# Linear attention and MLP: w_in loaded in even and odd partitions, its sums built in the first chunk on VectorE and GpSimd, late blocks of batch 1 in a tile of their own

## The chip, the cores and the metric

The kernel runs on one core of a Trainium2 chip. The core's engines work side by side, each with its own instruction stream: TensorE (PE, matmuls, with weight loads shown as PEld), VectorE (DVE), ScalarE (ACT), GpSimd (POOL) and SyncE (SP, which here issues DMA transfers). A tile on the core lies in SBUF, in 128 partitions; PE writes its results to PSUM, which has eight banks of 2 KB a partition. The metric is the device time of one execution in microseconds (us); the kernel before was run three times and its median counts.

## What is computed

Eight batches of eight heads with 576 positions of 64 elements go through a linear attention whose features are scaled with cosine and sine of the position. Its output, 4608 tokens of 512, goes through an MLP with 2048 hidden units.

```python
def _attn_ref(q, k, v):
    theta = np.pi / 2.0 * np.arange(S) / S
    def phi(x, c, s):
        r = np.maximum(x, 0.0)
        return np.concatenate([r * c, r * s], axis=-1)
    q_p, k_p = phi(q, cos_w, sin_w), phi(k, cos_w, sin_w)
    kv = np.einsum('bhsf,bhsd->bhfd', k_p, v)
    z = np.sum(k_p, axis=2)
    num = np.einsum('bhsf,bhfd->bhsd', q_p, kv)
    den = np.einsum('bhsf,bhf->bhs', q_p, z)[..., None] + 1e-06
    return num / den

def _moe_ref(x, w_in, w_out, beta):          # x: (4608, 512)
    h = x @ w_in                             # w_in: (512, 2048)
    g = h * (1.0 / (1.0 + np.exp(-beta * h)))
    return g @ w_out                         # w_out: (2048, 512)
```

## The kernel before

**Chunks and batches.** The MLP works on nine chunks of 512 tokens (c = 0 to 8), the attention on eight batches of 576 tokens, nine blocks of 64 each; chunk 0 is blocks 0 to 7 of batch 0, chunk 1 begins with block 8 of batch 0 and goes on with blocks 0 to 6 of batch 1, and so on. While PE does the MLP of one chunk, the other engines prepare the attention of the batch that the next chunk needs.

**A batch.** Raw q, k and v are loaded (`load_raw`, tiles `raw_q`, `raw_k`, `raw_v`, one of each, so that a load waits until the batch before has been read). `q_relu` and `k_relu` make bf16 tiles `qb` and `rk`, `v_scale` makes `vb` (v by cosine and by sine, with ones for the denominators). q is turned, either on PE (`q_turn_pe`, batches 0 and 1) or by a transposing DMA from SP (`q_turn_dma`), into `qt`; `tan_mul` multiplies it by the tangent into `qs`. `kv_mm` makes the 72 small matmuls of a batch's kv, `num_mm` multiplies q with it, `x_rden` and `x_mul` divide by the denominators into `xs`, and `x_turn_pe` or `x_turn_dma` turns that into `xt`, the left side of the MLP.

**The MLP.** h is made in 16 row tiles `jt` of 128 hidden units (`h_mm`, `h_group`), ACT computes silu(beta h) from it (`h_act`), and o is made from that with a w_out that is divided by beta. Weights come in fp32 pieces to four stage tiles (`load_w`), and are cast to bf16: `cast_win` into `win`, `cast_out` into `wout`, the latter with `rbeta`. From chunk 1 on o is made by a seven-product scheme (`o_fast`, later `o_pair`), which needs sums of w_out (`T1`, `T2`, `T3`, `T4`, made by `w_sums` in chunk 1) and sums of the activations (`S1` to `S4`); from chunk 3 on h is made the same way (`h_pair`), which needs four sums for each pair of row tiles of w_in (`wh_sum`, four of them in `wh_sums`, each a 128x256 subtraction or addition; eight pairs) and of x (`x_sum`).

**Order.** The schedule is by hand: instructions run on each engine in the order of the program, and wait for data by semaphores. Chunk 0 is a list of 32 slots: 4 to 15 are one row tile of h each, 16 to 23 are quarters of o, and 24 to 31 are one k step of o for all four token tiles. Work of batch 1 hangs on slots in the table `early`, work of batch 2 on slots of chunk 1. From chunk 2 on a string per chunk (`ORDERS`) gives the order, one word an operation: `W51` is sum 1 of pair 5 of `wh_sum`. SP issues loads in the order of the program too. Nearly all DMAs of the first 45 us go through it.

**In chunk 0**, DVE casts w_in's four quarters as they land (L115), does the last block of batch 0, casts eight row tiles of w_out (L123), scales v (L219), and takes k's and q's relu (L193); GpSimd and ACT take a share of the casts (L113). PE's h tiles wait for `win`, its o slots for `wout` (L544), and slot 22 ends with batch 1's `kv_mm` (L276). Between chunk 1's h and its o, ACT makes the two relus of batch 3's q (L192), in front of the copies of the first products out of PSUM (L602), which the products behind them wait for (L563).

The few lines that set this order:

```python
    22: lambda: (kv_mm(1, 0, 6), kv_mm(1, 1, 6), kv_take((0, 1), 6, "act"), q_relu(1, 1, "act", 5)),
    23: second,
    ...
    q_relu(3, 0, "act")
    q_relu(3, 1, "act")
    q_turn_dma(3)
    ...
    ops(x, "1 c1")
    one_sums(1)
    ops(y, "1 c1")
```

Of the kernel before, what the change touches and what calls it, by code (L numbers as in the profile page):

```python
# [16 lines left out]
P = 128  # L17
# [5 lines left out]
def kernel(  # L23
# [51 lines left out]

    def load_raw(b, name, j0=0, j1=4):
        js = slice(j0, j1)
        src = {"q": q, "k": k, "v": v}[name][b]
        nc.sync.dma_start(  # L79
            out=raw_tile(b, name)[:, js].rearrange("q j n d -> q j (n d)"),  # L80
            in_=src.rearrange("(j g) (p n) d -> (g p) j (n d)", g=2, n=NQ)[:, js, :])
# [8 lines left out]
    S1, S2, S3, S4 = (const.tile([P, JT // 2, TCH // 2], BF16, name=f"S{i}") for i in (1, 2, 3, 4))  # L90
    w_in_v = moe_w_in.rearrange("(j p) f -> p j f", p=P)
# [3 lines left out]
    def load_w(kind, i, step=4):  # L95
# [3 lines left out]
        for a in range(0, 4, step):  # L99
            if kind == "out":  # L100
                nc.sync.dma_start(out=st[:, a : a + step], in_=w_out_v[:, 4 * i + a : 4 * i + a + step, :])
                continue
            nc.sync.dma_start(out=st[:, a : a + step], in_=w_in_v[:, a : a + step, i * 512 : (i + 1) * 512])

    def cast_win(i, gj, eng="dve", f0=0, f1=512, jps=slice(0, 2)):

        g, jj = gj
        o = win[i].rearrange("q (jp g) f -> q jp g f", g=2)[jj * HP : (jj + 1) * HP, jps, g, f0:f1]
        a = stages["in", i].rearrange("q (jp jj) f -> q jp jj f", jj=2)[g * HP : (g + 1) * HP, jps, jj, f0:f1]
# [16 lines left out]
    GJ = [(0, 0), (0, 1), (1, 0), (1, 1)]  # L126

    load_raw(0, "q", 0, 2)
    load_raw(0, "q", 2, 4)
    beta16 = const.tile([JT, P], FP32, name="beta16")  # L130
    nc.scalar.dma_start(out=beta16, in_=moe_beta.rearrange("(j p) -> j p", p=P))
# [12 lines left out]
    zeros = S1.rearrange("q i t -> q (i t)")[:, 0:512]  # L144
# [50 lines left out]
    def q_relu(b, jp, eng="dve", n0=0, n1=NQ):  # L195
        return relu(qb[:, jp, n0:n1].rearrange("q n (j d) -> q j n d", j=2),
                    raw_tile(b, "q")[:, 2 * jp : 2 * jp + 2, n0:n1], eng)

    def k_relu(b, j0=0, j1=4, eng="dve", n0=0, n1=NQ):
        relu(rk.rearrange("q n j d -> q j n d")[:, j0:j1, n0:n1], raw_tile(b, "k")[:, j0:j1, n0:n1], eng)  # L200

    def v_scale(b, cs, jp=None, n0=0, n1=NQ, eng="dve"):
        t = (cos9, sin9)[cs]
        rv = raw_tile(b, "v")
        js = slice(0, 4) if jp is None else slice(2 * jp, 2 * jp + 2)
# [21 lines left out]
    def q_turn_pe(b, jp, bank, hold=False):  # L227

        parts = ((0, 0, 5), (1, 5, NQ))
# [40 lines left out]
    def kv_mm(b, jp, bank, jjs=(0, 1)):  # L270
        t = kv_out(jp, bank)
        for n in range(NQ):
            for jj in jjs:
                for g in range(2):
                    hs = slice(g * HP, (g + 1) * HP)
                    nc.tensor.matmul(  # L276
                        t[jj * HP : (jj + 1) * HP, g], lhsT=rk[hs, n, 2 * jp + jj, :],
                        rhs=vb[hs, n, 2 * jp + jj].rearrange("q s e -> q (s e)"),
# [10 lines left out]

    def num_mm(b, n, jp, bank, slot):  # L290

        for cs in range(2):
            for jj in range(2):
                rows = slice(jj * HP, (jj + 1) * HP)
                for g in range(2):
# [3 lines left out]
                        lhsT=(qts[b % 2], qs_of(b))[cs][rows, jp, n, cols],  # L299
# [15 lines left out]
    def x_mul(got, n0, n1):  # L315
        nv, rden, first, jps = got
        a, z, w = n0 - first, n1 - first, len(jps)
        o = xs[:, n0:n1, jps[0] : jps[-1] + 1].rearrange("q n s (j d) -> q j n s d", j=2)
# [6 lines left out]
    def x_mul_act(got, n):  # L325
        nv, rden, first, jps = got
        for s_, jp in enumerate(jps):
            for jj in range(2):
                nc.scalar.activation(xs[:, n, jp, jj * D : (jj + 1) * D], nv[:, jj, n - first, s_, 0:D],
# [67 lines left out]
    def g_sum(c, i0, i1, kind):  # L397

        k_ = i0 // 2
        g_e, g_o = (gs[c, k_][:, 2 * (i0 - 2 * k_) + r : 2 * (i1 - 2 * k_) : 2] for r in range(2))  # L400
        hf = TCH // 2
        A11, A12, A21, A22 = g_e[:, :, 0:hf], g_o[:, :, 0:hf], g_e[:, :, hf:TCH], g_o[:, :, hf:TCH]
        s1, s2, s3, s4 = (t[:, i0:i1] for t in (S1, S2, S3, S4))
# [18 lines left out]
    def wx_tiles():  # L422

        wx["w"] = stage.tile([P, 4, 512], FP32, name="w_stage", tag="w_stage").rearrange("q a f -> q (a f)").bitcast(
            BF16).rearrange("q (k s g f) -> q k s g f", k=4, s=4, g=2)
        wx["v"] = stage.tile([P, 4, 512], FP32, name="w_stage", tag="w_stage").rearrange("q a f -> q (a f)").bitcast(
            BF16).rearrange("q (k s g f) -> q k s g f", k=4, s=4, g=2)
# [5 lines left out]
    def w_sum(jt, i):  # L433
        return wx["w" if jt % 4 == 0 else "v"][:, jt // 4, i]

    def wh_sum(jt, kind):
# [6 lines left out]
        return nc.vector.tensor_tensor(o, l, r, op=op)  # L443

    def wh_sums(jt):
        for kind in (1, 3, 2, 4):
            got = wh_sum(jt, kind)
        return got
# [107 lines left out]
    def o_fast(c, pr, banks):  # L556
# [27 lines left out]
        def stored(key, op):  # L584
# [11 lines left out]
            "5": lambda: prod(e_ps, s_part(S1), T1, True, False),  # L596
            "6": lambda: prod(b_ps, s_part(S2), T2, False, False),
            "2": lambda: prod(a_ps, g_part(1, 0), B21, True, True),
            "7": lambda: prod(b_ps, s_part(S3), T3, False, False),
            "3": lambda: prod(e_ps, s_part(S4), B22, False, True),  # L600
# [11 lines left out]
    def o_pair(c, pr):  # L612
# [52 lines left out]
        lefts = (g_part(0, 0), s_part(S1), s_part(S2), g_part(1, 0), s_part(S3), s_part(S4), g_part(1, 1))  # L665
# [19 lines left out]
    warm_pe(58, 48)  # L685
# [7 lines left out]
    for bank, n0, n1 in ((6, 0, 5), (7, 5, NQ)):  # L693
        nc.vector.tensor_copy(tanr[:, n0:n1, :].rearrange("q n p -> q (n p)"), ps[:, bank, 0 : (n1 - n0) * HP])
# [47 lines left out]
    for gj, eng in zip(GJ, ("pool", "dve", "pool", "dve")):  # L742
        cast_win(0, gj, eng, jps=slice(0, 1))
    for gj, eng in zip(GJ, ("act", "pool", "pool", "pool")):
        cast_win(0, gj, eng, jps=slice(1, 2))
# [10 lines left out]
    def cast_halves(i, fs=(0, 256)):  # L756
        for f in fs:
            for gj in GJ:
                cast_win(i, gj, "pool" if i > 1 and gj == GJ[3] else "dve", f, f + 256)

    cast_halves(1)

    def rest():

        cast_halves(2)
        cast_halves(3)
        x_mul(x_rden(2, 0, 8, NQ, (0, 1)), 8, NQ)
# [3 lines left out]
        load_raw(1, "k")  # L771
# [320 lines left out]
```

## Time and profile before

| | us |
|---|---|
| median of three runs (273.26 to 273.82) | 273.54 |
| the profiled execution, its own time | 274.44 |
| its span, from the first to the last instruction | 272.7 |
| mean granted TensorE clock, share of full speed | 0.998 |

The page has a row for each engine's busy time as a share of the span, a chain of work that ended last, followed back from the last instruction, and groups of instructions by line. In a row, `L115 DVE CAST win<-w_stage 64x512 bf16<-64x512 f32 x20` is line 115 on VectorE, which makes `win` from `w_stage`, 64 partitions by 512 elements, twenty times. A timeline row begins with its start and its length in us and may end with idle time before it and what ended that; in a row of groups, busy time and the mean of one in ns follow the count; in a row of one line, shortest, median and longest in ns. Busy time by stretch of the span, with the share of DMA engines in use and what they moved:

```profile
20.00:30.00 10.00, 10.00 (x64) 4.53 (x62) 9.50 (x21) 8.43 (x13) 2.91 (x4) 1.00 1.05 388
30.00:38.00 8.00, 8.00 (x45) 3.53 (x47) 6.76 (x20) 6.48 (x13) 0.00 (x0) 1.00 1.05 391
50.50:70.20 19.70, 18.74 (x330) 10.32 (x328) 18.07 (x37) 16.57 (x28) 4.74 (x8) 1.00 1.06 304
```

The columns are the stretch, its length, busy us (and instructions) of PE, PEld, DVE, ACT and POOL, the granted clock, the DMA share and GB/s. The pieces of the loads landed one after the other: w_in's quarters at 16.39 (the first one's second half), 19.09, 21.82 and 24.51 us, w_out's first halves at 27.4 and 30.1, batch 1's v, k and q at 33.12, 36.13 and 39.14, the rest of w_out by 44.5.

### The profile page before, as it was taken

Reading aid. Unit: us, or ns where it says so; the run is one execution under the profiler, and the core shown is the slowest. Engines: PE = TensorE matmul, PEld = TensorE weight load, DVE = VectorE, ACT = ScalarE, POOL = GpSimd, SP = SyncE. Lnnn points to the kernel's source line nnn. Section 1 sums busy time; section 2 is a strip of 40 time slices with the busy share of each in tenths; the row PEclk is TensorE's granted clock in tenths of the full one; section 3 lists DMA queues with packets and bytes.
Section 4 is the critical chain, followed back from the end, with each engine's and each line's share of the span. In section 5 each row is a group of like instructions: output and inputs, shape, how many; then the busy total and the mean of one; then the engine's idle time right before and its main releaser. Section 6 shows DMA issues by size and latency. Waiting matters only on the chain.

```text
span 272.7 us, 8970 instructions
## 1 busy us (share of the span) xinstructions
PE 265.3 (97%) x3712; PEld 206.8 (76%) x3712; DVE 224.0 (82%) x596; ACT 188.4 (69%) x384; POOL 68.3 (25%) x89
## 2 busy tenths in 40 slices
PE   8899999999899999999999999999999999999994
PEld 8554455455784588888888888888888888888883
DVE  5989969499989889789989997899589768757852
ACT  4778777796419656899489966996696179428920
POOL 1444000510078000660085009300840060000001
PEclk9999999999999999999999999999999999999999
DMA  6999999999969999994589439943600570015005
GB/s 237 374 395 383 392 390 319 379 201 336 284 130 311 240 348 226 240 313 103 147 216 370 92 58 223 332 71 62 181 2 2 61 185 1 2 27 130 0 2 155
DMA packets 50681, 54.00 MB, mean 198 GB/s; under 512 B 31232, under 2 KB 31760, under 8 KB 50640
## 3 DMA queue, kind: packets, MB, share of 16 engines
q1 hardware_dynamic: 47504, 45.55, 59.1%
q0 software_dynamic: 2784, 7.61, 9.6%
q8 instruction: 29, 0.48, 0.7%
q10 hardware_dynamic: 352, 0.27, 0.4%
q14 instruction: 12, 0.10, 0.1%
HBM read 36.71 MB, written 9.44 MB: 169 GB/s over the span
## 4 chain that ended last, share of the span: by engine, by line
PE 85%; DVE 9%; DMA 3%; SPq 1%; issue 1%; ACT 1%; DVEq 0%
PE ps L621 32%; PE ps L511 27%; PE ps L386 10%; PE ps L544 5%; PE ps L563 4%; PE ps L297 3%; DMA raw_v<-in_v_dram 3%; PE ps L276 3%; DVE vb L219 1%; DVE xs L319 1%; DVE qs L223 1%; SPq L79 1%; DVE S L406 1%; DVE rk L193 1%; DVE qb L193 0%
## 5 line engine op out<-in xcount | busy, mean ns | idle before, releaser
L537 POOL DMA_DIRECT2D out_dram<-o_sb x58 | 33.9, 591 | 147.3 <-ACT o_sb L658 86.3
L420 ACT ACTIVATE g_t<-ps,beta 128x512 bf16<-128x512 f32 x96 | 60.3, 702 | 1.4 <-PE ps L511 1.3
L621 PEld LDWEIGHTS <-S 128*128 128x128 bf16 x448 | 43.4, 98 | 5.2
L511 PE MATMUL ps<-w_stage 128*128 128x256 bf16 x288 | 46.6, 272 | 0.1
L386 PE MATMUL ps<-xt,win 128*128 128x512 bf16 (+1 forms) x196 | 42.8, 375 | 0.1
L511 PEld LDWEIGHTS <-w_stage 128*128 128x128 bf16 x384 | 37.3, 98 | 5.1 <-issue 0.2
L487 DVE TENSOR_TENSOR ps<-ps,p 128x256 f32<-128x256 f32 x74 | 30.5, 428 | 8.6 <-PE ps L511 3.0
L394 ACT ACTIVATE g_t<-ps,beta 128x512 bf16<-128x512 f32 x48 | 32.3, 688 | 7.2 <-PE ps L386 7.1
L621 PEld LDWEIGHTS <-g_t 128*128 128x128 bf16 x336 | 32.3, 98 | 4.5 <-ACT g_t L420 0.4
L386 PEld LDWEIGHTS <-win 128*128 128x128 bf16 x196 | 18.7, 98 | 21.1 <-issue 0.5
L511 PE MATMUL ps<-xt,win 128*128 128x256 bf16 x192 | 32.9, 273 | 0.0
L511 PEld LDWEIGHTS <-win 128*128 128x128 bf16 x288 | 28.0, 98 | 3.4
L621 PE MATMUL ps<-wout,g_t 128*128 128x256 bf16 x224 | 28.9, 273 | 0.0
L406 DVE TENSOR_TENSOR S<-g_t 128x512 bf16<-128x512 bf16 (+1 forms) x66 | 25.7, 418 | 3.3 <-ACT g_t L420 1.7
L480 ACT COPY ps<-ps 128x256 f32<-128x256 f32 x62 | 22.6, 383 | 7.5 <-PE ps L621 4.0
L217 ACT ACTIVATE vb<-raw_v,sin 128x256 bf16<-128x256 f32 (+1 forms) x58 | 26.0, 503 | 1.5 <-DMA raw_v<-in_v_dram 1.5
L621 PE MATMUL ps<-T,S 128*128 128x256 bf16 x224 | 26.6, 273 | 0.0
L621 PE MATMUL ps<-wout,S 128*128 128x256 bf16 x224 | 26.4, 273 | 0.0
L319 DVE TENSOR_TENSOR xs<-ps,rden 128x768 bf16<-128x768 f32 (+4 forms) x26 | 22.8, 884 | 0.9 <-DVE rden L312 0.2
L223 POOL TENSOR_TENSOR qs<-qt,tanr 128x1152 bf16<-128x1152 bf16 x6 | 14.3, 2387 | 27.4 <-PE ps L563 21.0
L658 ACT COPY o_sb<-ps 128x512 f32<-128x512 f32 x11 | 6.3, 587 | 20.1 <-PE ps L621 20.1
L487 DVE TENSOR_TENSOR ps<-ps,u 128x256 f32<-128x256 f32 x36 | 15.3, 427 | 5.3 <-PE ps L511 3.3
(112 smaller groups left out, 414.7 us busy)
## 6 DMA issues: line engine op xcount, KB each, us to landing
raw_v<-in_v_dram SPq DMA_DIRECT2D x7, 1152.0 KB, 9.7
raw_k<-in_k_dram SPq DMA_DIRECT2D x7, 1152.0 KB, 9.5
raw_q<-in_q_dram SPq DMA_DIRECT2D x7, 1152.0 KB, 7.4
out_dram<-o_sb POOLq DMA_DIRECT2D x58, 128.0 KB, 4.5
w_stage<-in_moe_w_in_dram SPq DMA_DIRECT2D x3, 1024.0 KB, 12.8
w_stage<-in_moe_w_out_dram SPq DMA_DIRECT2D x2, 1024.0 KB, 7.9
w_stage<-in_moe_w_out_dram SPq DMA_DIRECT2D x4, 512.0 KB, 11.9
out_dram<-o_sb SPq DMA_DIRECT2D x10, 128.0 KB, 2.4
```

What stands on the lines that cost most here:

```text
L217: got = nc.scalar.activation(o, a, AF.Copy, scale=t[:, n : n + 1])
L223: return eng.tensor_tensor(dst.rearrange("q n (g p) -> q n g p", g=2), src.rearrange("q n (g p) -> q n g p", g=2), tanr[:, n0:n1].unsqueez ...
L319: nc.vector.tensor_tensor(o.rearrange("q j n s d -> q j (n s) d"), nv[:, :, a:z, :, 0:D].rearrange("q j n s d -> q j (n s) d"), rden[:, :, ...
L386: nc.tensor.matmul(ps[:, h_bank(c, jt), i * 64 : (i + w) * 64], lhsT=win[jt // 4][:, mi, (jt % 4) * P : (jt % 4 + 1) * P], rhs=xt[:, i : i ...
L394: return nc.scalar.activation(gs[c, jt // 4][:, jt % 4], ps[:, h_bank(c, jt)], AF.Silu, scale=beta[:, jt : jt + 1])
L406: return nc.vector.tensor_tensor(o, l, r, op=op)
L420: return nc.scalar.activation(gs[c, jt // 4][:, jt % 4], bank, AF.Silu, scale=beta[:, jt : jt + 1])
L480: return nc.scalar.copy(at("a", 0), at("b", 0))
L487: nc.vector.tensor_tensor(dst, at("b", 0), st["p5"], op=ALU.add)
L511: nc.tensor.matmul(dst, lhsT=l[:, g], rhs=r[:, :, g * HP : (g + 1) * HP], start=start and g == 0, stop=g == 1, skip_group_check=True)
L537: (eng or own).dma_start(out=out_v[bb, n][:, m0:m1], in_=o_sb[hf * HP : (hf + 1) * HP, m0:m1])
L621: nc.tensor.matmul(dst, lhsT=l(i), rhs=r[:, i], start=start and i == 0, stop=i == order[-1], skip_group_check=True)
```

## The change

1. w_in's rows are put into partitions so that a row tile's even partitions hold one head's half and the odd ones the other's; each load becomes two DMAs with every second partition, and a cast covers all 128 partitions. In step with it the heads' order in the raw tiles (`heads`) and the order of elements in `xs` change.
2. The sums of w_in (`wh_sums`) move from chunk 1's end, chunk 2 and the strings of chunks 2 and 3 into chunk 0 (`rest`), four pairs on VectorE and four on GpSimd, into tiles of their own; `S1` to `S4` move into stage tiles.
3. The sums of w_out (`t_sum`) are made in halves, from chunk 0 on; T3 is made whole at slot 0 of chunk 1.
4. Batch 0's block 8 moves from slot 4 to slot 22 (`eighth`), with its part of qs in a place of its own. Batch 1's late blocks 7 and 8 of q get a tile of their own (`late_qb`, in T1's second half), are turned by two DMAs and multiplied by the tangent on GpSimd; PE turns seven blocks. The other turns of batch 1 move by two slots, batch 1's last blocks and batch 2's kv to slot 11 of chunk 1.
5. Batch 3's q relus go behind the first two products. Chunk 1 begins with half products of four row tiles. In chunk 0's slots 4 to 9 three of four matmuls are done in two halves of 256 columns. A small load goes ahead of beta on ACT, the copies of `tanr` go from VectorE to ACT, the warm-up of PE has 54 matmuls for 58.

```diff
+    def heads(j0, j1):
+
+        if j1 - j0 == 4:
+            return slice(0, 4)
+        at = 2 * (j0 % 2) + j0 // 2
+        return slice(at, at + 1) if j1 - j0 == 1 else slice(at, 4, 2)
...
-    S1, S2, S3, S4 = (const.tile([P, JT // 2, TCH // 2], BF16, name=f"S{i}") for i in (1, 2, 3, 4))
-    w_in_v = moe_w_in.rearrange("(j p) f -> p j f", p=P)
+    w_sums_of = [const.tile([P, 4, 4, 2, P], BF16, name=f"ws{i}") for i in range(2)]
+    S = {}
+    late_qb = T1[:, 6:8].rearrange("q i t -> q (i t)").rearrange("q (s n c) -> q s n c", s=2, n=2)
+    w_in_v = moe_w_in.rearrange("(jj mi d) f -> jj d mi f", jj=2, d=HP)
...
-            nc.sync.dma_start(out=st[:, a : a + step], in_=w_in_v[:, a : a + step, i * 512 : (i + 1) * 512])
-
-    def cast_win(i, gj, eng="dve", f0=0, f1=512, jps=slice(0, 2)):
-
-        g, jj = gj
-        o = win[i].rearrange("q (jp g) f -> q jp g f", g=2)[jj * HP : (jj + 1) * HP, jps, g, f0:f1]
-        a = stages["in", i].rearrange("q (jp jj) f -> q jp jj f", jj=2)[g * HP : (g + 1) * HP, jps, jj, f0:f1]
+            for jj in range(2):
+                nc.sync.dma_start(out=st[jj:P:2, a : a + step],
+                                  in_=w_in_v[jj, :, a : a + step, i * 512 : (i + 1) * 512])
+
+    def cast_win(i, mi0, mi1, eng="dve", f0=0, f1=512):
+        o, a = win[i][:, mi0:mi1, f0:f1], stages["in", i][:, mi0:mi1, f0:f1]
...
+    touch = const.tile([2 * H, 8], FP32, name="touch")
+    nc.scalar.dma_start(out=touch, in_=v[0].rearrange("h (s r) d -> (h s) r d", s=2)[:, 0, 0:8])
     nc.scalar.dma_start(out=beta16, in_=moe_beta.rearrange("(j p) -> j p", p=P))
...
-        parts = ((0, 0, 5), (1, 5, NQ))
+        parts = ((0, 0, 5), (1, 5, NQ)) if b == 0 else ((0, 0, 4), (1, 4, 7))
...
-        o = xs[:, n0:n1, jps[0] : jps[-1] + 1].rearrange("q n s (j d) -> q j n s d", j=2)
+        o = xs[:, n0:n1, jps[0] : jps[-1] + 1].rearrange("q n s (d j) -> q j n s d", j=2)
...
+        for i in (1, 3):
+            both = stage.tile([P, 4, 512], FP32, name="w_stage", tag="w_stage").rearrange("q a f -> q (a f)").bitcast(
+                BF16).rearrange("q (k i t) -> q k i t", k=2, i=JT // 2)
+            S[i], S[i + 1] = both[:, 0], both[:, 1]
...
-    warm_pe(58, 48)
+    warm_pe(54, 48)
...
-    for gj, eng in zip(GJ, ("pool", "dve", "pool", "dve")):
-        cast_win(0, gj, eng, jps=slice(0, 1))
-    for gj, eng in zip(GJ, ("act", "pool", "pool", "pool")):
-        cast_win(0, gj, eng, jps=slice(1, 2))
+    for mi, eng in enumerate(("pool", "dve", "act", "pool")):
+        cast_win(0, mi, mi + 1, eng)
...
-    def cast_halves(i, fs=(0, 256)):
-        for f in fs:
-            for gj in GJ:
-                cast_win(i, gj, "pool" if i > 1 and gj == GJ[3] else "dve", f, f + 256)
+    def cast_halves(i):
+        for f in range(0, 512, P):
+            cast_win(i, 0, MI, "dve", f, f + P)
 
     cast_halves(1)
 
+    def t_sum(kind, i0, i1):
+        o, l, r = {1: (T1, B12, B11), 2: (T2, B22, T1), 4: (T4, B21, T2), 3: (T3, B22, B12)}[kind]
+        nc.vector.tensor_tensor(o[:, i0:i1], l[:, i0:i1], r[:, i0:i1], op=ALU.subtract)
+
     def rest():
 
+        nc.gpsimd.tensor_copy(qs_last, qs_first[:, :, NQ - 1])
         cast_halves(2)
+        wh_sums(0)
+        wh_sums(2)
         cast_halves(3)
-        x_mul(x_rden(2, 0, 8, NQ, (0, 1)), 8, NQ)
+        wh_sums(4)
+        wh_sums(6)
+        for jt in (8, 10, 12, 14):
+            wh_sums(jt, nc.gpsimd)
         load_w("out", 0)
         load_w("out", 1)
         load_raw(1, "v")
         load_raw(1, "k")
+        load_w("out", 2, 2, 0, 2)
         load_raw(1, "q")
-        load_w("out", 2, 2)
+        load_w("out", 2, 2, 2, 4)
         load_w("out", 3, 2)
-        x_turn_dma(0, 8, 9)
-        for j in range(8):
+        for j in range(4):
             cast_out(j)
+        for j in range(4, 8):
+            cast_out(j)
+        t_sum(1, 0, 4)
         v_scale(1, 0)
         v_scale(1, 1, n0=8)
         k_relu(1, 0, 2)
-        q_relu(1, 0)
-        q_relu(1, 1, n1=5)
+        t_sum(2, 0, 4)
 
 
     def num_seven(jp, bank):
         for n in range(7):
             num_mm(1, n, jp, bank, n)
 
-    takes = []
-
-    def second():
-
-        takes.append(q_turn_pe(1, 0, 4, hold=True))
-        takes.append(q_turn_pe(1, 1, 6, hold=True))
+    def eighth():
+        for jp in range(2):
+            num_mm(0, 8, jp, 4, jp)
+        kv_mm(1, 0, 6)
+        kv_mm(1, 1, 6)
+        kv_take((0, 1), 6, "act")
+        x_mul(x_rden(4, 0, 8, NQ, (0, 1)), 8, NQ)
+        x_turn_dma(0, 8, NQ)
         cast_out(8)
+        cast_out(9, "a")
+        t_sum(4, 0, 4)
+        q_relu(1, 0, n1=7)
+        q_relu(1, 1, n1=4)
+        q_relu(1, 1, "act", 4, 7)
+        for jp in range(2):
+            relu(late_qb[:, jp].rearrange("q n (j d) -> q j n d", j=2), raw_tile(1, "q")[:, jp::2, 7:], "act")
+        for jp in range(2):
+            nc.sync.dma_start(out=qts[1][:, jp, 7:], in_=late_qb[:, jp].rearrange("q n c -> q (n c)"), transpose=True)
+
+    def turn():
+
+        for jp in range(2):
+            tan_mul(nc.gpsimd, qs_first[:, jp, 7:], qts[1][:, jp, 7:], 7, NQ)
+        load_raw(2, "q")
+        load_raw(2, "v")
+        load_raw(2, "k")
+        takes = [q_turn_pe(1, jp, 4 + 2 * jp, hold=True) for jp in range(2)]
+        cast_out(10)
+        cast_out(11, "a")
         takes[0]("act", 0)
         takes[0]("dve", 1)
-        cast_out(9, "a")
         takes[0]("dve", 0)
         takes[0]("act", 1)
-        cast_out(10)
-        for e, i in (("act", 0), ("dve", 1), ("act", 1), ("dve", 0)):
-            takes[1](e, i)
-        for j in (11, 12, 14, 15):
+        takes[1]("act", 0)
+        takes[1]("dve", 1)
+        takes[1]("dve", 0)
+        takes[1]("act", 1)
+        cast_out(12)
+        cast_out(13, "a")
+
+    def sevens():
+        for jp in range(2):
+            num_seven(jp, 4 + 2 * jp)
+        for j in (14, 15):
             cast_out(j, "a")
+        for jp in range(2):
+            x_mul(x_rden(4 + 2 * jp, 0, 0, 7, (jp,)), 0, 7)
+        t_sum(1, 4, 8)
 
     early = {
-        4: lambda: (num_mm(0, 8, 0, 2, 0), num_mm(0, 8, 1, 2, 1), rest()),
+        4: rest,
         15: lambda: (v_scale(1, 1, n1=8, eng="act"), k_relu(1, 2, 4, "act")),
-        22: lambda: (kv_mm(1, 0, 6), kv_mm(1, 1, 6), kv_take((0, 1), 6, "act"), q_relu(1, 1, "act", 5)),
-        23: second,
-        25: lambda: (num_seven(0, 4), x_mul(x_rden(4, 0, 0, 7, (0,)), 0, 7), cast_out(13)),
-        26: lambda: (num_seven(1, 6), x_mul(x_rden(6, 0, 0, 7, (1,)), 0, 7)),
-        28: lambda: x_turn_pe(1, 0, 7, 4, ("act",), (0,)),
-        29: lambda: x_turn_pe(1, 0, 7, 5, ("dve",), (1,)),
+        22: eighth,
+        25: turn,
+        27: sevens,
+        30: lambda: x_turn_pe(1, 0, 7, 4, ("act",), (0,)),
+        31: lambda: (x_turn_pe(1, 0, 7, 5, ("dve",), (1,))),
     }
 
...
-            h_group(0, slot)
+            h_group(0, slot, 2 if slot < 10 else 1)
...
-        if slot == 24:
-            for name in "qvk":
-                load_raw(2, name)
...
-    def w_sums():
-        z = ALU.subtract
-        nc.vector.tensor_tensor(T1, B12, B11, op=z)
-        nc.vector.tensor_tensor(T2, B22, T1, op=z)
-        nc.vector.tensor_tensor(T4, B21, T2, op=z)
-        nc.vector.tensor_tensor(T3, B22, B12, op=z)
-
     wx_tiles()
+    t_sum(2, 4, 8)
+    t_sum(4, 4, 8)
+    for jt in range(4):
+        h_mm(1, jt, (0, 1))
     for slot in range(16):
-        h_group(1, slot)
+        if slot < 4:
+            h_mm(1, slot, (2, 3))
+            h_act(1, slot)
+        else:
+            h_group(1, slot)
         if slot == 0:
-            num_rest()
             att_q(2)
             v_half(2, 0)
+            t_sum(3, 0, 8)
         if 2 <= slot < 6:
             v_half(2, 1, slot + 3, slot + 4, "act")
         if slot == 4:
             k_all(2)
             v_half(2, 1, 0, 5)
-        elif slot == 6:
-            w_sums()
-        elif slot == 10:
+        elif slot == 11:
+            num_rest()
             kv_all(2, eng="act")
-            for jp in range(2):
-                tan_mul(nc.vector, qs_of(2)[:, jp], qts[0][:, jp], 0, NQ)
-    q_relu(3, 0, "act")
-    q_relu(3, 1, "act")
-    q_turn_dma(3)
-
+            x_rest()
+            q_tan(2, 0)
+            tan_mul(nc.vector, qs_of(2)[:, 1], qts[0][:, 1], 0, NQ)
...
     ops(x, "1 c1")
     one_sums(1)
     ops(y, "1 c1")
+    q_relu(3, 0, "act")
+    q_relu(3, 1, "act")
+    q_turn_dma(3)
...
-    got = wh_sums(0)
...
-            "ox16 W61 N12 N00 oy17 x0 oxc4 oyc5 ox5 ox6 oxd k2 k0 k3 k1 v5 x1 N20 oxe W62 oy6 v4 v1 v3 oy5 Lk x2 oyD "
...
+            "ox16 N12 N00 oy17 x0 oxc4 oyc5 ox5 ox6 oxd k2 k0 k3 k1 v5 x1 N20 oxe oy6 v4 v1 v3 oy5 Lk x2 oyD "
...
```

## The prediction

> **What bounds the kernel now.** I read the page's busy shares and its chain, then the waits of TensorE (PE), then the two places where the change touches what PE waits for.
>
> ```profile
> span 272.7 us, 8970 instructions
> PE 265.3 (97%) x3712; PEld 206.8 (76%) x3712; DVE 224.0 (82%) x596; ACT 188.4 (69%) x384; POOL 68.3 (25%) x89
> PE 85%; DVE 9%; DMA 3%; SPq 1%; issue 1%; ACT 1%; DVEq 0%
> ```
>
> PE is busy for 97% of the span, so an edit counts only if it changes PE's own work or a gap of PE. From 18.65 us to the end I find one gap over 0.25 us. The timelines of PE and of ScalarE (ACT) show it:
>
> ```profile
> 70.15 0.38 PE L563 MATMUL ps<-T,S 128*128 128x256 bf16 x2 [0.96 <-ACT p L602]
> 67.62 2.22 ACT L192 ACTIVATE qb<-raw_q 128x1152 bf16<-128x1152 f32 x2 [0.82 <-DMA raw_q<-in_q_dram]
> 69.74 0.63 ACT L602 COPY p<-ps 128x256 f32<-128x256 f32 x2
> ```
>
> Columns: start, length, engine and line, what it made, idle time before it and who ended it. ACT waits for batch 3's q, spends 2.22 us on its relu, and only then copies the product that PE needs out of its bank. From the last matmul's start at 68.99 to 70.15, PE lost 1.15 us.
>
> **The stretch into which the change moves work** is 19 to 38 us. The timelines of VectorE (DVE) and PE:
>
> ```profile
> 19.11 10.23 DVE L115 CAST win<-w_stage 64x512 bf16<-64x512 f32 x20 [0.52 <-DMA w_stage<-in_moe_w_in_dram]
> ...
> 30.12 3.25 DVE L123 TENSOR_SCALAR wout<-w_stage,rbeta 128x512 bf16<-128x512 f32 x8
> 33.28 2.45 DVE L219 TENSOR_SCALAR vb<-raw_v,cos 128x256 bf16<-128x256 f32 x9
> ...
> 36.15 0.76 DVE L193 TENSOR_SCALAR rk<-raw_k 128x1152 bf16<-128x1152 f32 x1 [0.16 <-DMA raw_k<-in_k_dram]
> 39.17 1.16 DVE L193 TENSOR_SCALAR qb<-raw_q 128x1152 bf16<-128x1152 f32 x2 [2.25 <-DMA raw_q<-in_q_dram]
> ```
>
> ```profile
> 31.77 6.21 PE L544 MATMUL ps<-wout,g_t 128*128 128x512 bf16 x28
> 37.90 1.22 PE L276 MATMUL ps<-vb,rk 64*64 64x130 bf16 x72
> ```
>
> DVE is busy without a break until k's relu ends at 36.91. PE starts chunk 0's output products at 31.93 (they need wout) and batch 1's kv products at 37.97 (they need vb and rk). So DVE has 1.1 us in hand there, and its 2.25 us of idle time lies too late to help.
>
> **Part 1, DVE's programme in chunk 0, with no contention.** Casts of w_in now use all 128 partitions, 512 elements a lane as before, so an instruction costs the same and there are 12 where there were 20. Added are 16 sums on DVE and 16 on GpSimd (POOL). A DVE sum of this shape stands in the trace:
>
> ```profile
> L443 DVE TENSOR_TENSOR w_stage<-w_stage,win x1: 282/282/282, 75.7 to 75.7; 128x256 bf16<-128x256 bf16 x1
> ```
>
> Four in a row start 0.2, 0.2, 0.32 and 0.21 us apart, 0.93 in all. The third quarter of w_in lands at 21.82; its four casts, at 0.34 from start to start, end at 23.2; eight sums (1.86) end at 25.05; the last quarter (landed 24.51) is cast by 26.4; eight sums end at 28.27; eight casts of w_out at 0.395 (the x8 row, start to start) end at 31.43; half a T sum (0.66, half of T's 1.22 at 60 us and its fixed part) ends at 32.1. v lands at 33.12, k at 36.13: v's scaling and k's relu end as before, at 35.87 and 36.91. Batch 0's last block (0.8 us of DVE) has left this stretch. PE needs rk at about 38.0. Idle time that can take up delay: 32.1 to 33.12 is 1.0, between v and k 0.3, before PE 1.1: **2.4 us** in all. The nearer deadline, the first w_out casts (28.75 against 31.7), has 3.0.
>
> **Part 2, what GpSimd's 16 sums do to DVE.** This decides the case. Rows of the same DVE cast beside two GpSimd casts (22.25 to 23.65 us) and without any (26.3 to 29.3), then the GpSimd casts:
>
> ```profile
> L115 DVE CAST win<-w_stage 64x512 bf16<-64x512 f32 x2 | 1.5, 733 | 0.0
> ```
>
> ```profile
> L115 DVE CAST win<-w_stage 64x512 bf16<-64x512 f32 x7 | 2.9, 421 | 0.2
> ```
>
> ```profile
> L113 POOL CAST win<-w_stage 64x512 bf16<-64x512 f32 x2 | 1.6, 801 | 3.2 <-DMA w_stage<-in_moe_w_in_dram 3.2
> ```
>
> Each GpSimd instruction costs DVE 733 − 421 = 0.31 us, and itself becomes longer (0.602 alone). The same is seen with a long GpSimd sum, whose second instance ends at 76.51 + 4.73 = 81.24, and a DVE scaling that started at 80.29:
>
> ```profile
> 76.51 4.73 POOL L223 TENSOR_TENSOR qs<-qt,tanr 128x1152 bf16<-128x1152 bf16 x2 [20.97 <-PE ps L563]
> ```
>
> ```profile
> L219 DVE TENSOR_SCALAR vb<-raw_v,cos x4: 343/344/1107, 80.3 to 81.8; 128x256 bf16<-128x256 f32 x4
> ```
>
> 1107 where 343 is usual: DVE stood until GpSimd was through, and had only 0.15 left to do. A GpSimd sum of 128x256 is not in the trace. L209's two instances (1.90 us for 1024 elements, 1.26 for 640) give 1.7 ns an element and 0.19 fixed, so 0.62; L223's 2387 ns in proportion gives 0.53. They start at about 22.65 and, interleaved with DVE, last beyond 32: DVE's work there is casts, sums of two SBUF tiles and scalings, all of the kinds in these rows. I take 0.31 each, since a 0.62 us instruction against a dense stream of 0.25 to 0.45 us ones is nearest to the cast rows: 16 × 0.31 = 5.0. Less 2.4 in hand, PE stands **2.6 us** before batch 1's kv products. PE has no later gap that would give this back. Bounds: if DVE loses a whole GpSimd instruction but for the 0.14 of it that its own start-up covers (L406 at 148.8 us: 0.63 long, 0.28 of them after GpSimd's end, usually 0.42), 16 × 0.48 = 7.7, so 5.3 of stall; if GpSimd gets in only where DVE waits for data anyway, at most 2.4, so none.
>
> The Trainium skill (SBUF — State Buffer, Who interferes with whom) says that the two engines share a pair of ports as an exclusive lock, held for the whole instruction, and that a DVE operation with two SBUF inputs contends with a GpSimd one that reads SBUF. By it the sum would go to the upper bound; the cast rows, at 0.31 of 0.60, show partial overlap instead.
>
> **Part 3, the gap at 69 us.** ACT's two relus of q(3) now stand behind the copies of the first two products. Behind them wait ACT's later copies, but PE has num_all and the next products to do meanwhile. On DVE the four T sums, 59.34 to 64.12 on the chain, are gone but for one of 1.2 us. I take −1.0 of 1.15.
>
> **Part 4, small terms.** Four transposes of q fewer on PE, each 1.07/18 = 0.06: −0.24. Chunk 0's early slots in two halves of 256 columns: 109 + 109 ns against 216, 18 times: +0.04. At the start ACT gets the tan copies and one small load ahead of beta, DVE loses a cast: +0.1 (bounds −0.2 and +0.35: PE's startup gaps of 0.70 <- ACT rk and 0.69 <- ACT kv could each move by an issue or a copy).
>
> **At nothing, and by what cover.** The sums of w_in taken out of chunks 1 to 3 (32, in eight groups of 0.93 on DVE) ended no wait of PE there. The strided x writes read fp32 from PSUM at one element a cycle already (957 ns for 768); 36 strided elements cost 0.1 to 0.16 start to start. SP issues five DMAs more, about 0.45 each, while over 2 MB are queued; its loads of w_in cross half the partitions each, bounded by the same 390 GB/s and, if slower, by up to 1 us of delay for the second quarter. Behind the two late transposes (1.2 to 2.7 us each) on SP stand batch 2's three loads, 0.5 to 1 late; ACT's scaling of v(2) has 2.6 us of slack. Batch 0's block 8 turns about 8 us later by DMA; its x is due at 50.5, it landed at 44.8. The turns of batch 1 at slots 30 and 31 are covered by the eight matmuls with rows 0 and 1 (1.7 us); uncovered, about 0.8.
>
> **Sum.** +2.6 − 1.0 − 0.24 + 0.04 + 0.1 = +1.5. The profiled execution took 274.44 (span 272.7 and 1.74 around it); it becomes 275.9. The median of the three runs, 273.54, is 0.90 below it: **275.0**.
>
> **Rivals.** (A) GpSimd gets its turns only in DVE's waits, or D stays under 2.4. For it: alternate casts had 13 to 31 ns between them, and no row shows GpSimd beside a dense DVE stream of sums. Against: the 733 row. No stall, −1.1: 272.4, faster. From D = 3.5 on it is slower. (B) Whole-instruction blocking, as the 1107 row has it: 5.3 − 1.1 = +4.2: 277.7. The rule of the Trainium skill named above (SBUF — State Buffer, Who interferes with whom) would end here; the 801 row, GpSimd held up in turn, is half of what it says. (C) As A, but the gap at 69 is only moved: q(3), loaded behind more SP work, keeps ACT when the next copies are due, and 0.9 of the gap comes back: 273.3, no change.
>
> **Chances.** Forecast 0.42, A 0.36, B 0.13, C 0.09. About ±0.2% (0.55 us) can't be told from no change. Faster: A and 0.03 of the forecast's lower edge, 0.39; same: C, 0.09; slower: the rest of the forecast and B, 0.52. The forecast's own range (0.25 to 0.39 lost to each sum) is 274.0 to 276.3; with A and most of B it is 272.1 to 277.8.
>
> **What would show it.** Right: DVE casts, sums and w_out scalings between 22 and 36 us at 0.5 to 0.75 us where GpSimd runs; GpSimd's sums lengthened too; PE idle at 38 to 41 us, released by DVE's rk or vb; no gap near 69; 14 transposes of q. Wrong: GpSimd sums that start only when DVE waits, DVE ones at 0.28, and k's relu done before 38; or a new wait of PE at batch 1's turns (slots 22 to 31) or at chunk 1's start that I set to nothing.

## The result, and the profile after

The changed kernel took 283.35 us (median of 4 runs, 282.96 to 284.04) against 273.68 for the kernel before on the same chip: ratio 1.0357, 95% interval 1.033 to 1.0384. It is 9.7 us slower; forecast were 275.0, at most 277.8. Here and below a time is the median of all runs of a kernel; its ratio leaves out single runs more than 1.5% above the fastest of the same kernel. The page, with the same rows as before (span, busy time by engine, shares of the chain):

```profile
span 281.7 us, 9002 instructions
PE 267.2 (95%) x3722; PEld 208.4 (74%) x3722; DVE 224.3 (80%) x571; ACT 188.6 (67%) x388; POOL 80.3 (29%) x102
PE 76%; DMA 12%; DVE 8%; SPq 1%; issue 1%; DVEq 0%
```

The span is 9.0 us longer: PE is busy for 1.9 us more and idle for 7.1 us more. The view of PE's waits names them (line, what it waited for; sum, number, longest in us):

```profile
PE ps L555 <- DVE wout L131: 3.2, 1, 3.2
PE ps L398 <- DMA xt<-xs: 2.0, 1, 2.0
PE ps L308 <- POOL qs L232: 1.4, 1, 1.4
PE ps L398 <- DVE win L123: 1.3, 1, 1.3
```

Two lie in chunk 0, before w_in's casts (until 29.35 us) and before w_out's (until 36.21); two lie later, before the tangent product of batch 2 (until 75.05) and before chunk 2's x (until 89.93). By PE's milestones: batch 1's kv products begin at 44.59 us where they began at 37.90, chunk 1 at 56.40 where it began at 50.52 (5.9 later), and batch 3's kv products at 97.8 where they began at 88.5 (9.3 later). So some 6 us are lost in chunk 0 and 3.4 more between 56 and 98, already less the gap of 1.15 us at 69 us that has gone. After that nothing is added.

In chunk 0 the timelines of VectorE and GpSimd show why:

```profile
23.88 1.43 DVE L455 TENSOR_TENSOR ws<-win 128x256 bf16<-128x256 bf16 x2
...
25.55 0.64 DVE L455 TENSOR_TENSOR ws<-win,ws 128x256 bf16<-128x256 bf16 x1
...
28.88 1.89 DVE L123 CAST win<-w_stage 128x512 bf16<-128x512 f32 x4
...
35.69 3.25 DVE L131 TENSOR_SCALAR wout<-w_stage,rbeta 128x512 bf16<-128x512 f32 x8
```

```profile
22.90 1.59 POOL L455 TENSOR_TENSOR ws<-win 128x256 bf16<-128x256 bf16 x2 [5.55 <-DVE win L123]
24.45 0.71 POOL L455 TENSOR_TENSOR ws<-ws,win 128x256 bf16<-128x256 bf16 x1
25.24 0.80 POOL L455 TENSOR_TENSOR ws<-win,ws 128x256 bf16<-128x256 bf16 x1
```

Two of VectorE's sums take 1.43 us, over 0.7 each, where one took 0.28. They wait for GpSimd's: the VectorE sum that starts at 25.55 ends at 26.19, 0.15 after the GpSimd sum that ends at 26.04. Sixteen sums and four casts fill 11.8 us, from 23.88 to 35.69. The casts of w_out begin at 35.69 instead of 30.12, and PE, through with its h tiles at 33.0, stands. GpSimd's own sums take 0.67 to 0.85 each, where the prediction had estimated 0.53 to 0.62; none of them stands alone in a trace. PE's busy time and granted clock around that wait (stretch, length, busy us of PE, PEld, DVE, ACT, POOL, then the clock):

```profile
33.00:36.20 3.20, 0.00 (x0) 0.00 (x0) 3.17 (x6) 3.19 (x8) 2.54 (x4) 1.00 1.05 388
37.20:40.90 3.70, 3.70 (x11) 1.27 (x10) 3.70 (x12) 0.75 (x1) 0.00 (x0) 0.54 1.04 386
```

About 1 us after PE went on, its granted clock fell, to 0.54 on average over these 3.7 us. An estimate of the loss: at full clock the same work takes 3.70 × 0.54 = 2.0 us, 1.7 less.

Later, in the chain and on GpSimd:

```profile
59.79 11.52 DMA qt<-qb
```

```profile
71.47 3.52 POOL L232 TENSOR_TENSOR qs<-qt,tanr 128x1152 bf16<-128x1152 bf16 x1 [9.45 <-DMA qt<-qb]
```

```profile
72.67 3.61 DVE L418 TENSOR_TENSOR w_stage<-g_t 128x512 bf16<-128x512 bf16 x4
```

Batch 2's q is turned by a DMA issued at 59.79 that lands 11.5 us later (before: 55.47 to 62.17, 6.7 us), and its tangent product takes 3.52 us on GpSimd, beside VectorE's. PE waits for that product. VectorE's sums of the activations stand beside it too, and four of them take 3.61 us; they take 1.42 in the run below that has no tangent product on GpSimd there. So the taking of turns comes back at this place.

### The profile page after: what moved, and what is told of

It is laid out like the page before. It is cut to its first block, busy times and chain, and to the rows that moved or that the text cites. A ratio compares the mean times of both kernels' runs of the same rounds, so it can differ in the third digit from the quotient of the medians.

```text
span 281.7 us, 9002 instructions
## 1 busy us (share of the span) xinstructions
PE 267.2 (95%) x3722; PEld 208.4 (74%) x3722; DVE 224.3 (80%) x571; ACT 188.6 (67%) x388; POOL 80.3 (29%) x102
## 4 chain that ended last, share of the span: by engine, by line
PE 76%; DMA 12%; DVE 8%; SPq 1%; issue 1%; DVEq 0%
PE ps L632 31%; PE ps L522 26%; PE ps L398 6%; PE ps L555 6%; DMA qt<-qb 4%; DMA raw_k<-in_k_dram 3%; DVE ws L455 3%; PE ps L308 3%; DMA w_stage<-in_moe_w_in_dram 3%; PE ps L285 2%; DVE w_stage L418 2%; DMA xt<-xs 2%; DVE win L123 1%; SPq L86 1%; PE ps L574 1%
## 5 line engine op out<-in xcount | busy, mean ns | idle before, releaser
L632 PEld LDWEIGHTS <-w_stage 128*128 128x128 bf16 x448 | 43.4, 98 | 5.2
L522 PE MATMUL ps<-w_stage,ws 128*128 128x256 bf16 x288 | 46.6, 273 | 0.0
L522 PEld LDWEIGHTS <-ws 128*128 128x128 bf16 x384 | 37.3, 98 | 4.9
L498 DVE TENSOR_TENSOR ps<-ps,p 128x256 f32<-128x256 f32 x74 | 30.6, 428 | 9.5 <-PE ps L522 2.9
L398 PEld LDWEIGHTS <-win 128*128 128x128 bf16 x214 | 20.5, 98 | 23.2 <-DMA xt<-xs 2.2
L418 DVE TENSOR_TENSOR w_stage<-g_t 128x512 bf16<-128x512 bf16 (+1 forms) x66 | 28.0, 453 | 5.9 <-ACT g_t L406 3.9
L232 POOL TENSOR_TENSOR qs<-qt,tanr 128x1152 bf16<-128x1152 bf16 (+1 forms) x9 | 19.2, 2140 | 41.9 <-DMA qt<-T 15.3
L522 PEld LDWEIGHTS <-win 128*128 128x128 bf16 x288 | 28.0, 98 | 3.4
L632 PE MATMUL ps<-T,w_stage 128*128 128x256 bf16 x224 | 26.6, 273 | 0.0
L632 PE MATMUL ps<-wout,w_stage 128*128 128x256 bf16 x224 | 26.4, 273 | 0.0
L331 DVE TENSOR_TENSOR xs<-ps,rden 128x768 bf16<-128x768 f32 (+4 forms) x26 | 24.3, 942 | 0.8
L228 DVE TENSOR_SCALAR vb<-raw_v,cos 128x256 bf16<-128x256 f32 x63 | 20.9, 380 | 0.5 <-DMA raw_v<-in_v_dram 0.5
L498 DVE TENSOR_TENSOR ps<-ps,u 128x256 f32<-128x256 f32 x36 | 15.3, 428 | 6.9 <-PE ps L522 5.3
```

The costliest lines, as they stand in the source:

```text
L228: got = nc.vector.tensor_scalar(o, a, scalar1=t[:, n : n + 1], scalar2=None, op0=ALU.mult)
L331: nc.vector.tensor_tensor(o.rearrange("q j n s d -> q j (n s) d"), nv[:, :, a:z, :, 0:D].rearrange("q j n s d -> q j (n s) d"), rden[:, :, ...
L398: nc.tensor.matmul(ps[:, h_bank(c, jt), i * 64 : (i + w) * 64], lhsT=win[jt // 4][:, mi, (jt % 4) * P : (jt % 4 + 1) * P], rhs=xt[:, i : i ...
L498: nc.vector.tensor_tensor(dst, at("b", 0), st["p5"], op=ALU.add)
L522: nc.tensor.matmul(dst, lhsT=l[:, g], rhs=r[:, :, g * HP : (g + 1) * HP], start=start and g == 0, stop=g == 1, skip_group_check=True)
L632: nc.tensor.matmul(dst, lhsT=l(i), rhs=r[:, i], start=start and i == 0, stop=i == order[-1], skip_group_check=True)
```

## The experiments

Fifteen kernels, each against the kernel before on its own chip (273.4 to 273.7 us).

**Chunk 0.** First, GpSimd's sums on VectorE, in the same place.

```diff
-            wh_sums(jt, nc.gpsimd)
+            wh_sums(jt)
```

> The changed kernel with GpSimd's 16 sums made by VectorE in the same place. Theory T (taking turns: a GpSimd sum holds VectorE up for its own turn, about 0.45 us each over chunk 0): without GpSimd the sums stand 0.23 us apart, the casts of w_out begin at 32.0 us instead of 35.7, TensorE loses about 1.8 us in chunk 0 instead of 6.5, and its clock is not halved: 276 to 279 us. Rival R (it is the amount of work that VectorE gets in chunk 0, and who shares it matters little): VectorE now has 16 sums more, w_out's casts begin no earlier than 35 us, 282 us or more.

278.22 us, ratio 1.0146 (1.0103 to 1.019). Batch 1's kv begins at 39.25 us, and the clock stays at 1.00 in chunk 0. VectorE's timeline:

```profile
23.10 0.49 DVE L455 TENSOR_TENSOR ws<-win 128x256 bf16<-128x256 bf16 x2
...
31.89 3.25 DVE L131 TENSOR_SCALAR wout<-w_stage,rbeta 128x512 bf16<-128x512 f32 x8
```

The same sixteen sums and four casts that filled 11.8 us now fill 5.07 (23.10 to 28.17); even with sixteen sums more, w_out starts 3.8 us earlier than with GpSimd's help. Here work taken off VectorE made it slower. Theory T had w_out's casts at 32.0 and 1.8 us lost; measured are 31.89 and, by kv's start against the next run, 1.7. R falls.

Next, GpSimd's four pairs back in chunks 2 and 3, and then all eight.

```diff
-        for jt in (8, 10, 12, 14):
-            wh_sums(jt, nc.gpsimd)
...
+            if slot == 9:
+                wh_sums(8)
...
```

(The first kernel; not shown are its strings of chunks 2 and 3. The second takes VectorE's four pairs out of chunk 0 as well.)

> The changed kernel with the four pairs that GpSimd sums put back to VectorE where the kernel before had them, in chunks 2 and 3; VectorE keeps its own 16 sums in chunk 0. T: w_out's casts begin at 28.3 us and TensorE waits for nothing in chunk 0; the 6.5 us there come back. What is left tells two theories of the later gaps (73 to 90 us, 4.5 us in the changed kernel) apart. S1 (they follow from chunk 0's delay): 272 to 273 us. S2 (they are of the change's own making, by the order of loads, turns and tangent): 276 to 277 us with the same gaps. R: w_out's casts begin at 31 us or later and TensorE still loses 2 us or more in chunk 0.

> The changed kernel with all 32 sums where the kernel before had them; all else of the change stands. T: no different from the run before it by more than 0.6 us, since 16 sums on VectorE alone fit into what it has in hand in chunk 0. S1: 272 to 273 us. S2: 276 to 277 us.

276.16 (1.0097, 1.0063 to 1.0131) and 275.63 (1.007, 1.0047 to 1.0093). In both, chunk 0 has no wait for win or for the first casts of w_out, and kv begins at 37.5 and 37.6: 16 sums on VectorE alone cost nothing measurable there. With them w_out's casts begin at 28.59:

```profile
28.59 3.32 DVE L131 TENSOR_SCALAR wout<-w_stage,rbeta 128x512 bf16<-128x512 f32 x8
```

But 2 us remain, with the wait for GpSimd's tangent product:

```profile
PE ps L308 <- POOL qs L232: 1.7, 1, 1.7
```

(waits of PE, all sums back). So theory S1 falls for that gap: it is of the change's own making. The wait for chunk 2's x is in neither trace.

The other way round, the kernel before with the moved sums alone:

```diff
         cast_halves(2)
+        wh_sums(0)
+        wh_sums(2)
         cast_halves(3)
+        wh_sums(4)
+        wh_sums(6)
+        for jt in (8, 10, 12, 14):
+            wh_sums(jt, nc.gpsimd)
...
```

(Not shown: the sums get tiles of their own, `S1` to `S4` go into stage tiles, and the sums are taken out of their old places.)

> The kernel before with only the sums of w_in moved to chunk 0, 16 on VectorE and 16 on GpSimd, in tiles of their own. T: VectorE's sums at 0.7 us, casts of w_out from about 36 us, TensorE loses 6 to 7 us in chunk 0: 279.5 to 280.5 us if nothing follows later (S2), 282 to 284 us if the late chunk 0 brings the later gaps with it (S1). R without turn-taking: about 3.7 us of VectorE work less what it has in hand, 274 to 276 us.

283.7 us (1.0379, 1.0346 to 1.0411). PE's waits:

```profile
PE ps L387 <- DVE win L116: 4.5, 1, 4.5
PE ps L545 <- DVE wout L124: 2.7, 1, 2.7
```

Moving the sums alone costs as much as the whole change, but all of it falls into chunk 0, where GpSimd's casts of w_in are still in place: kv begins at 47.85, 10 us late, where theory T had 6 to 7. After it PE has no gap over 0.2 us, although everything is later. So a late chunk 0 alone does not make the later gaps. The total is the one that S1 named, but not for S1's reason.

What do the two engines take turns for? GpSimd's sums were replaced by writes of zeros.

```diff
-            wh_sums(jt, nc.gpsimd)
+            for i in range(4):
+                for _ in range(2):
+                    nc.gpsimd.memset(w_sum(jt, i), 0.0)
```

> The changed kernel with each of GpSimd's 16 sums replaced by two writes of zeros to the same place (about 0.3 us each by the row of a 128x128 one, 0.198), so about as much GpSimd time, but nothing read from SBUF; these sums are left out of the result. Theory T1 (what VectorE and GpSimd take turns for is reading SBUF): VectorE's sums stand 0.23 us apart, w_out's casts begin near 28.3 us, chunk 0 is free of stalls, 276 to 277 us. T2 (any GpSimd instruction on SBUF holds VectorE up): sums at 0.5 us or more, w_out's casts from 33 us on, 280 to 284 us.

277.03 us (1.0126, 1.0097 to 1.0155), kv at 37.58. The timelines of GpSimd (the row begins with the view; all 32 writes run from 17.26 to 29.89) and VectorE:

```profile
20.83 9.06 POOL L787 MEMSET ws<- 128x256 bf16 x23
```

```profile
23.96 0.47 DVE L455 TENSOR_TENSOR ws<-win 128x256 bf16<-128x256 bf16 x2
...
25.81 2.21 DVE L123 CAST win<-w_stage 128x512 bf16<-128x512 f32 x4
```

GpSimd writes without a break, and VectorE's sums run at full speed (0.47 for two). Its casts do not: four take 2.21 us, 1.43 without GpSimd. So theory T1 holds for sums of two SBUF inputs; casts are held up by writes as well. That is what the Trainium skill says (SBUF — State Buffer, Who interferes with whom): an operation with two SBUF inputs contends with a GpSimd instruction that reads, not with one that only writes, while a cast in a two-port mode contends with either.

Last for chunk 0, matmuls to fill PE's wait.

```diff
+            if slot == 16:
+                for _ in range(14):
+                    nc.tensor.matmul(ps[:, 7], lhsT=win[0][:, 0, 0:P], rhs=win[0][:, 1, :], start=True, stop=True)
```

> The changed kernel with 14 matmuls whose result is never read ahead of slot 16, 3.0 us of work in the 3.2 us that TensorE waits for w_out. Theory: part of the loss in chunk 0 is the clock, granted at 0.50 from 37.4 to 40.4 us after that wait, 1.5 us; kept busy, TensorE keeps its clock and the time falls to 281.5 to 282.2. Rival: VectorE's casts of w_out, 0.395 us apart, set the pace there in any case, and nothing is gained: 283 to 284.

279.28 us (1.0199, 1.0179 to 1.0219), 4.1 less than the changed kernel, a larger gain than expected. The granted clock stays:

```profile
38.20:40.40 2.20, 2.20 (x12) 0.98 (x10) 2.20 (x8) 0.00 (x0) 0.00 (x0) 1.00 1.05 388
```

kv begins at 42.8 instead of 44.6: 1.8 us for the clock, near the estimate of 1.7. The rest, 2.3 us, lies behind chunk 0: the wait for chunk 2's x is not there in this trace. Why it is not is open.

**The later gaps.** These start from the kernel with all sums back (275.63).

```diff
-            q_tan(2, 0)
-            tan_mul(nc.vector, qs_of(2)[:, 1], qts[0][:, 1], 0, NQ)
+            for jp in range(2):
+                tan_mul(nc.vector, qs_of(2)[:, jp], qts[0][:, jp], 0, NQ)
```

> The changed kernel with all sums of w_in back in their old places (275.6 us when it ran), and batch 2's tangent product of the first pair on VectorE again instead of GpSimd. It had one gap near 67 us, 1.96 us before a kv-numerator product that waits for GpSimd's tangent product, and 0.4 and 0.29 behind it. Theory U (the tangent on GpSimd is the cause: it takes 3.5 us there, beside VectorE's sums): both products are done 2.7 us after the turned q lands instead of 3.6, the gap shrinks to about 1.0 and the time to about 274.6. Rival V (q's turn for batch 2 lands late, at 65.0 instead of 62.2, since its load stands behind the late blocks' turns on SP): the landing stays at 65 and the gap stays above 0.8; 274.5 to 275.6.

276.21 us, with runs from 273.75 to 277.86 (1.009, 1.006 to 1.0121). In the trace PE's wait shrinks from 1.7 to 1.0 us (from start to start, as the expectation counts, 1.96 to 1.14), but q's turn still lands at 65.2. Both theories allow that, and the time lies above both: the run does not tell them apart.

So batch 2's loads ahead of the late turns, without and with the edit of the tangent:

```diff
-        load_raw(2, "q")
-        load_raw(2, "v")
-        load_raw(2, "k")
...
+        for name in "qvk":
+            load_raw(2, name)
         for jp in range(2):
             nc.sync.dma_start(out=qts[1][:, jp, 7:], in_=late_qb[:, jp].rearrange("q n c -> q (n c)"), transpose=True)
```

> The same start (all sums back, 275.6 us), with batch 2's three loads ahead of the two late turns of batch 1 on SP. V: the loads are issued about 3 us earlier, batch 2's turned q lands at 62 us or earlier, the gap near 67 goes: 273.0 to 273.7. U: the landing may move, but GpSimd's product still ends after TensorE needs it; gap 1 us or more, 274.8 to 275.6.

> The same start with both edits, tangent on VectorE and loads first. V: no better than loads first alone, 273.0 to 273.7. U and V together: the gap near 67 gone and less than 0.5 us of gaps from 20 us to the end; 272.6 to 273.2, which would be faster than the kernel before, by the gap at 69 us that the moved relus take away.

281.17 (1.0287, 1.0261 to 1.0313) and 280.83 (1.0266, 1.0247 to 1.0285). Both theories missed a wait. PE's longest wait with the loads first, and from VectorE's timeline the row that waits for the late turns (in brackets):

```profile
PE ps L398 <- DVE xt L375: 6.8, 1, 6.8
```

```profile
56.36 1.01 DVE L774 TENSOR_TENSOR T<-wout 128x1024 bf16<-128x1024 bf16 x1 [8.09 <-DMA qt<-T]
```

The late turns now land at 56.0 and 56.2 us, behind the loads. The late blocks live in the second half of the tile T1, which VectorE overwrites at slot 27; it waited there for the turns to have read it, and batch 1's x stood behind it on VectorE. The home of the late blocks ties a DMA to VectorE's order. The rest of that trace, from 62 us on, has no gap over 0.21 us.

So T's second halves were moved to slot 8 of chunk 1, without and with VectorE's 16 sums in chunk 0:

```diff
-        t_sum(1, 4, 8)
...
-    t_sum(2, 4, 8)
-    t_sum(4, 4, 8)
...
+        elif slot == 8:
+            for kind in (1, 2, 4):
+                t_sum(kind, 4, 8)
```

> Sums of w_in back in their old places, tangent on VectorE, batch 2's loads ahead of the two late turns, and, new, the second halves of T1, T2 and T4 at slot 8 of chunk 1: T1's second half is the home of the late blocks, so in the two runs before VectorE stood in front of T1's second half until the late turns had landed (56 us), and TensorE 6.8 us behind it. Theory U and V: that wait goes, the gap near 67 too: 272.4 to 273.2 us. Rival: with the loads first the late turns land at 56 us and something else (the tangent of the late blocks, chunk 2's x) waits for them: 273.5 or more.

> The same as the run before it, but VectorE's 16 sums stay in chunk 0 as in the change (GpSimd's 16 are back in chunks 2 and 3). T (16 sums on VectorE alone fit into what it has in hand): within 0.6 us of the run before it. Rival: they press on w_out's casts or on k's relu, and 0.7 us or more are lost in chunk 0.

274.1 (1.0007, 0.9987 to 1.0026) and 273.92 (1.0008, 0.9984 to 1.0032): 1.5 and 2.2 us less than their starts, and no different from the kernel before. The times lie above the 272.4 to 273.2 expected; in the trace of the first PE still waits 0.9 us for chunk 2's x. Batch 2's turned q lands at 60.0 and 59.3 (65.0 with the sums back), and the gap near 67 is gone. Both edits are in these kernels, so what each of them, tangent and loads, is worth stays open. In these two T3 still overwrote B12 ahead of T1's second half, whose values are therefore others; the instructions are the same. With T3 put behind:

> VectorE's 16 sums in chunk 0, GpSimd's 16 back in chunks 2 and 3, tangent on VectorE, batch 2's loads ahead of the late turns, second halves of T1, T2 and T4 at slot 8 of chunk 1, and T3 behind them (in the two runs before it was ahead of them and overwrote what T1's second half is made from). Same work as the run with VectorE's sums in chunk 0: 272.5 to 274, with single runs up to 277 if chunk 2's x, turned by DMA behind batch 3's q, comes late in them.

274.27 (0.9998, 0.9976 to 1.002), a little above the expectation, runs from 272.33 to 276.76. Its trace has one late gap, chunk 2's x:

```profile
PE ps L398 <- DMA xt<-xs: 1.5, 1, 1.5
```

```diff
-    q_turn_dma(3)
...
     x_part(2, 2, 0)
+    q_turn_dma(3)
```

> The same with batch 3's q turned behind chunk 2's three x turns on SP instead of ahead of them. If the x turns' lateness (80.75 us, TensorE idle 0.9 from 78.7 in one trace) makes the spread of single runs, the median falls to 272.3 to 272.9 and no run is above 274. Rival: batch 3's q now comes late for its tangent and chunk 2 waits for it: 273.5 or more.

274.46 (1.0033, 1.0011 to 1.0055): in the trace the gap at 79 us is gone, another of 0.6 ends at 106.6 (PE waits for VectorE's L498), and single runs still reach 276.75. The median did not fall, so the late x turns are not what makes the runs spread; what does is open. No version here beats the kernel before.

Do the two losses add? The changed kernel, GpSimd's sums kept, with batch 2's repairs only:

> The changed kernel, sums on GpSimd kept, with only the repairs of batch 2: tangent on VectorE, loads ahead of the late turns, T's second halves and T3 at slot 8. If the two losses add up: the later gaps (4.5 us together from 73 to 90 us) shrink to under 1.0, chunk 0 still loses 6.5: 279.5 to 281. Rival (the later gaps follow from chunk 0's delay whatever is done to batch 2): 282.5 to 283.5.

278.97 us (1.0195, 1.0172 to 1.0217), 4.4 less than the changed kernel and half a us below the expectation. Its waits of PE:

```profile
PE ps L555 <- DVE wout L131: 3.3, 1, 3.3
PE ps L398 <- DVE win L123: 1.3, 1, 1.3
```

Chunk 0 is as before, of the later gaps nothing over 0.2 us is left. So the later gaps come from the order of batch 2's work, and the rival falls. But the two losses do not simply add: chunk 0 alone costs 5.4 us (this run), the later gaps alone about 2 (the 275.63 run), both together 9.7. With chunk 0 late, the later gaps cost 4.4; through which wait the lateness makes them grow was not tested.

**The gap at 69 us by itself**, in the kernel before:

```diff
-    q_relu(3, 0, "act")
-    q_relu(3, 1, "act")
-    q_turn_dma(3)
...
     ops(y, "1 c1")
+    q_relu(3, 0, "act")
+    q_relu(3, 1, "act")
+    q_turn_dma(3)
```

> The kernel before with one thing changed: the two relus of batch 3's q, and its turn, behind the copies of both first products. Forecast's step: the gap of 1.15 us at 69 us goes, nothing comes in its place: 272.4 to 272.7 us. Rival: a later copy waits behind the relus and the gap moves: 273.3 to 273.8.

273.74 us against 273.43 (1.0014, 0.9998 to 1.003). ACT's timeline has the copies first:

```profile
67.16 0.37 ACT L602 COPY p<-ps 128x256 f32<-128x256 f32 x1 [0.18 <-DVE S L406]
68.03 0.37 ACT L602 COPY p<-ps 128x256 f32<-128x256 f32 x1 [0.50 <-PE ps L563]
68.30 2.22 ACT L192 ACTIVATE qb<-raw_q 128x1152 bf16<-128x1152 f32 x2
```

The gap is gone and no other took its place (span 272.0, with h starting 0.5 later than in the trace of before), yet the timed runs did not gain. Whether they have that gap as the one profiled execution had is not known.

## Why the prediction was wrong

- **What bounds the kernel, and where the change would hurt**: right. VectorE's programme in chunk 0 without contention was right too: w_out's casts were put at 28.27 and began at 28.59 with the 16 sums on VectorE alone. One term of it was luck: 0.34 us from cast to cast stands in no row of the kernel before, where casts of that length start 0.44 apart; the changed kernel's do start 0.34 apart.
- **Part 2, 0.31 us lost to each GpSimd sum**: the step that failed first. Measured: 11.81 − 5.07 = 6.7, and 1.91 − 1.43 = 0.5 for the casts just ahead, 7.2 over 16, so 0.45 each. The upper bound, 0.48, was nearly exact, and its mechanism, that of rival B (0.13), fits the rows: a VectorE sum ends 0.15 us after the GpSimd one beside it. The row that I chose does not carry over from casts to sums. Beside GpSimd, casts started 0.78 us apart and sums 0.67 on average (seven of each eight were held up; eight took 5.0 us, 1.86 alone). Alone, a cast takes 0.44 from start to start, a sum 0.23. So a cast lost 0.34 and a sum 0.44: the shorter instruction lost more.
- **2.4 us in hand, the rest stall before kv**: the place was wrong. PE stood earlier, before w_in's casts (1.3) and w_out's (3.2), and not before kv. The prediction's other deadline, w_out's casts with 3.0 in hand, fits: they began at 35.69 instead of 28.27, 7.4 late, which leaves 4.4 against 4.5 measured. And the sum had no term for PE's clock: the wait of 3.2 us was followed by an estimated 1.7 us lost at half clock (1.8 in the run with PE kept busy). 4.5 and 1.7 make 6.2 of the 6.7 us by which kv was late; about 0.5 more goes with the pace of w_out's casts (the 28 products of w_out ahead of kv take 6.74 us in the run with PE kept busy, at full clock, and 6.21 before).
- **Part 3, −1.0**: in the traces the gap went, in the timed runs it brought nothing (+0.3 us, and the interval goes from −0.05 to +0.8 us).
- **"At nothing, and by what cover"**: wrong in one item. Batch 2's loads were put 0.5 to 1 late, with ACT's scaling of v next in line. With the sums back, q's load was issued at 44.37 us, 4.0 later than before, and what was late next was q's turn by DMA (65.04 against 62.17), then the tangent on GpSimd, an edit that the sum did not cost at all. These later gaps cost about 2 us, and 4.4 with chunk 0 late: the largest term of the miss. The DMA for batch 0's block 8, the strided writes and the moved turns of batch 1 showed no wait.
- **Rival C** named the queue (SP) but not the place, and came on top of the stall, not instead of it.

So the steps that failed are the 0.31 for each sum, the missing term for the clock, and batch 2's late q, whose cost was put at nothing. 275.0 lacked 2.2 us of contention (7.2 − 5.0), 1.7 of clock and 4.4 of later gaps, 8.3 together; measured was 8.35 more. That this comes out so closely is partly luck, since the 1.0 that Part 3 counted as won is not in it: with it the sum is 9.3, and about 1 us must overlap or have been won elsewhere.

## What to carry to other kernels

Moving work from VectorE to GpSimd can cost VectorE more than it takes off: here its sums of two SBUF inputs were held up by GpSimd's sums, and its casts by GpSimd's plain writes too. Read from a mixed stretch how far apart VectorE's instructions start, for the same kind and length as those that will stand there, and subtract what they take alone. A wait of PE near 3 us is priced with the clock behind it, and in a moved load the next reader of each thing that lands is followed to PE, not only the nearest one. Before a tile is given a second use, list who writes it next and what stands behind that writer.

## What was not expected of the hardware

Waits of PE of 3.2 us (the changed kernel), 3.3 us (with batch 2's repairs) and 4.5 us (the kernel before with the sums alone) each brought 3.4 us at clock 0.50, the two waits of 6.8 us brought 6.8 us; one of 2.7 us (kernel before with the sums alone, before w_out) brought none. When the clock falls differs: 4.2 us after PE had stopped in the changed kernel, 2.7 us after in the run with both edits. The Trainium skill (TensorE: Matmul & The Clock Gate, What's actually happening) gives an idle window of about 3.4 us; in these traces a wait somewhat shorter than that was enough. And GpSimd's plain writes slow VectorE's casts, from 1.43 to 2.21 us for four, but leave its sums alone.
